# Eight weight places opened in the order in which their memory is freed, and one weight load of mid-stream split into 24 and 104 partitions

## The chip, the cores and the metric

The kernel runs on one core of one Trainium2 chip. The metric is the device time of one execution in microseconds; lower is better. A kernel is timed in several runs, and the profile is one more execution of the same program, taken by the hardware profiler. A verdict of "faster" or "slower" needs 2%.

Engine names in the profile: PE is the matmul engine, PEld its weight loads, DVE and ACT the vector and scalar engines, POOL the engine that issues nearly all loads here, SP another issuing engine. "L115" is line 115 of the kernel. The changed kernel has two more lines, so L546 and L551 of before are L548 and L553 of after.

## The reference

The reference is banded attention (8 heads, window 64) on 8 sequences of 576 rows, then a mix in the frequency domain, then a channel mix with a residual. The part that matters here is the middle one: 64 modes, each with a real and an imaginary 512 x 512 weight matrix.

```python
    X = np.fft.rfft(x, axis=1)
    ...
    Xr, Xi = (np.real(X[:, :n_modes]), np.imag(X[:, :n_modes]))
    Yr = np.einsum('bmd,mde->bme', Xr, w_r) - np.einsum('bmd,mde->bme', Xi, w_i)
    Yi = np.einsum('bmd,mde->bme', Xr, w_i) + np.einsum('bmd,mde->bme', Xi, w_r)
    Y[:, :n_modes] = Yr + 1j * Yi
    y = np.fft.irfft(Y, n=S, axis=1)
    u = x + y
    return (u + np.maximum(u @ w_ch, 0.0)).astype(np.float32)
```

All 127 weight matrices that are used (the imaginary one of mode 0 is not) have to be read once. They are most of the traffic.

## The kernel before

A weight load brings one matrix into a tile of 128 partitions and casts it to bf16 on the way. POOL issues it:

```python
    NLOAD = 2 * NM - 1            # 127
    def mode_of(i):               # the mode that load i belongs to
        return (i + 1) // 2

    def load_w(i, pool, tag, wt=None):
        m, im = divmod(i + (i > 0), 2)
        if wt is None:
            wt = pool.tile([128, NC, DM], BF16, name="wt", tag=tag)
        src = moe_w_i if im else moe_w_r
        nc.gpsimd.dma_start(out=wt, in_=src[m].rearrange("(p c) e -> p c e", c=NC))
        wtiles[m, im] = wt
```

During attention, the first 18 matrices go to places of their own (5 in a pool "wl", 13 in a pool "we", which the attention phase's memory holds), and more go to tiles that attention has finished with. When attention ends, its memory is given to other tiles. Eight of the new tiles are the "wm" places, which lie where "we" matrices and other tiles of the first phase lay. A place can be loaded only when what lay there has been read for the last time. `opens` says after which mode each place is offered to the stream of loads, and places are used in the order in which they come free:

```python
    MW = 8
    wmid = p2.enter_context(tc.tile_pool(name="wmid", bufs=1, side="right", reuse_waits="tile"))
    ...
    for j in range(LW):
        opens.setdefault(mode_of(j), []).append(("wl", j, NM))
    for j in range(MW):
        at = mode_of(LW + 6 + j) if LW + 6 + j < EARLY else vt_mode
        opens.setdefault(at, []).append(("wm", j, M0 + 2 * (j // 2)))
    free = []

    def refill_w(m):
        nonlocal nw
        for i in (2 * m - 1, 2 * m):
            if i in slot_of:
                free.append(slot_of.pop(i))
        free.extend(opens.pop(m, []))
        while nw < NLOAD and free:
            kind, j, last = slot = free.pop(0)
            if mode_of(nw) >= last:
                continue
            ...                    # load_w(nw, ...) into that place
            slot_of[nw] = slot
            nw += 1
```

POOL issues in program order. If the first load of a row of loads has to wait for its place, those behind it wait as well, even where their own places are free (13.85 us in the trace shown below).

The softmax here doesn't subtract the row's maximum and nothing guards it: scores larger than these inputs give would overflow.

## Time and profile before

| | before |
|---|---|
| median of the runs | 430.43 us (430.21 to 431.14) |
| the profiled execution | 431.61 us, 1.2 us above the median |
| bytes moved, mean rate | 92.18 MB, 214 GB/s |
| pace of the loads in mid-stream | one 512 KB weight load every 2.46 us |
| last weight landing | 392.41 us (from the DMA completions in the trace) |

The first view is the page of the kernel before. The DMA and GB/s rows cut the span into 40 slices; a digit 9 means that the sixteen DMA engines were busy for 90% of the slice or more. The queue lines give packets, megabytes, and the time that the packets took as a share of sixteen engines' span. The two groups are the mode matmuls: busy time and mean length, then the idle time just before them and what ended most of it.

```profile
DMA  7999999999999999999999999999999999993898
GB/s 140 213 215 211 213 213 211 213 213 213 214 213 213 198 210 231 212 213 214 213 213 213 213 213 213 214 213 214 213 213 213 213 214 213 213 214 73 265 344 292
DMA packets 31104, 92.18 MB, mean 214 GB/s; under 512 B 3424, under 2 KB 3680, under 8 KB 31056
...
q0 software_dynamic: 25984, 82.55, 96.6%
q8 instruction: 39, 0.64, 0.5%
...
L551 PE MATMUL psy<-XQ,wt 128*128 128x16 bf16 x784 | 48.1, 191 | 46.6 <-DMA wt<-in_moe_w_i_dram 44.0
L546 PE MATMUL psy<-XQ,wt 128*128 128x16 bf16 x832 | 52.1, 191 | 31.5 <-DMA wt<-in_moe_w_r_dram 31.0
```

From 3 to 390 us the DMA stream runs at 213 GB/s in nearly every slice, and the mode matmuls were kept idle for 44.0 + 31.0 = 75.0 us by weights that had not landed. So the stream of loads is the bound. The queue q8 carries instruction fetches: 39 of them, 16 KB each. They take 0.5% of the engines' time.

The second view is the table of windows of the kernel before: start and end, length, busy time and count of PE, PEld, DVE, ACT and POOL, then the granted clock, the DMA share, and GB/s.

```profile
core 0: us, PE busy (x) PEld busy (x) DVE busy (x) ACT busy (x) POOL busy (x), PEclk, DMA share, GB/s
168.00:171.00 3.00, 1.70 (x60) 1.58 (x55) 0.42 (x1) 1.17 (x2) 2.29 (x5) 0.50 0.78 182
171.00:390.00 219.00, 135.75 (x1871) 103.45 (x1872) 47.27 (x111) 34.40 (x66) 45.11 (x87) 0.69 1.06 213
343.00:352.00 9.00, 5.89 (x80) 4.43 (x80) 1.37 (x2) 1.16 (x2) 3.18 (x7) 0.67 1.07 215
392.50:430.00 37.50, 27.67 (x128) 20.13 (x128) 25.00 (x40) 24.34 (x47) 9.10 (x18) 0.92 0.76 259
```

The stream's usual share is 1.06 (a row takes 0.324 us and the next one starts 0.3045 us after it, so a full engine counts slightly over 1). At 168 to 171 us it falls to 0.78. The third view, the timeline of POOL in the kernel before, shows why. The bracket at the end of a line is the idle time before it and what ended it.

```profile
154.11 0.75 POOL L585 DMA_DIRECT2D wch<-in_moe_w_ch_dram  x1 [0.66 <-PE psy L546]
168.71 0.53 POOL L115 DMA_DIRECT2D wt<-in_moe_w_i_dram  x1 [13.85 <-PE psy L551]
169.23 0.54 POOL L115 DMA_DIRECT2D wt<-in_moe_w_r_dram  x1
169.75 0.55 POOL L115 DMA_DIRECT2D wt<-in_moe_w_i_dram  x1
...
172.35 0.59 POOL L115 DMA_DIRECT2D wt<-in_moe_w_r_dram  x1
```

After the load of `wch` nothing is issued for 13.85 us, because the load into the place wm0 waits for PE; the seven loads behind it then go out at once. The loads in flight run out meanwhile: from 170.0 to 170.5 us the DMA share is 0.48.

The fourth view is the timeline of PE at the end of the weight stream: the last two matrices, each multiplied as soon as it has landed.

```profile
389.98 0.63 PE L729 MATMUL psl<-XQ,wt 128*128 128x16 bf16 x16 [0.44 <-DMA wt<-in_moe_w_r_dram]
392.45 0.65 PE L729 MATMUL psl<-XQ,wt 128*128 128x16 bf16 x16 [0.47 <-DMA wt<-in_moe_w_i_dram]
```

PE waits for the last landing. Whatever makes that landing earlier makes the kernel shorter; the 37.4 us of the span after it are the last rows and the output.

### A finer clock: sixteen landings for each load

A load counts as landed when its semaphore has risen by sixteen: in the trace of before, each of the 120 starts of PE or PEld that a load had held up comes 0.04 us or more after the sixteenth increment of that load (median 0.04 us). The trace records sixteen increments for every load, spread over 0.71 us (the load landing at 173.68 us) to 3.66 us (the one landing at 123.64 us). A weight load has 128 rows of 4,096 bytes. In the packet list they fall into sixteen sequences side by side, each of 8 rows and a small write of 4 bytes for every load; such a sequence is taken as one engine here. Rows of one engine start 0.3045 us apart and the small write takes 0.022 us, so the 8 rows and the write make the 2.46 us.

The packets of the instruction fetches stand among these rows. In the trace of before the one at 243.11 us lies between two rows of one engine, and the next of them starts 0.96 us after it. The lengths of the 39 repeat with period eight (945, 936, 975, 974, 961, 893, 893 and 948 ns; 36 of 39 within 2 ns), which fits eight engines hit in turn. In the increments the sixteen do fall into two groups of eight: for the load landing at 340.77 us, eight lie within 0.66 us of the first and the other eight 1.54 to 3.00 us behind it. These are called the fast and the slow engines below. That the fetches are what makes these slow is inferred from these numbers.

This document uses one derived number. For each of the sixteen increments, "behind schedule" is its time less the time at which it would have come if every load so far had taken 2.457 us (2.795 us for one of q, k or v, 2.60 us for `wch`). The mean of the sixteen tells how the stream is doing; the largest tells when the load has landed. The trace does not name the engine of a packet, so the engines are numbered here in the order in which a load's rows are dealt to them.

### The profile page before, as it was taken

How to read it: one execution, taken by the hardware profiler on the slowest of the kernel's cores; microseconds unless marked ns; L12 is line 12 of the kernel's file. 1: busy time of each engine (PE TensorE's matmuls, PEld its weight loads, DVE VectorE, ACT ScalarE, POOL GpSimd, SP SyncE). 2: the span in 40 equal slices, each digit the busy share in tenths (PEclk: the TensorE clock that was granted, in tenths of full speed). 3: DMA queues.
4: the chain of work that ended last, by engine and by line, in shares of the span. 5: the costliest groups of instructions: out<-in, count | busy, mean ns of one | idle time of the engine just before them, and what ended most of it. 6: DMA issues, size and time to landing. Idle time of an engine off the chain costs nothing.

```text
span 429.8 us, 11338 instructions
## 1 busy us (share of the span) xinstructions
PE 316.0 (74%) x5057; PEld 228.0 (53%) x5057; DVE 162.0 (38%) x317; ACT 154.6 (36%) x271; POOL 98.3 (23%) x188
## 2 busy tenths in 40 slices
PE   6999999999989776422678888877266652398892
PEld 5665665666654476311566665655244541364681
DVE  5466766666662200306232322212011110042893
ACT  4585866866763121001122222122011110032891
POOL 7131321231020132221121221211111032101510
PEclk9999999999995555555598988879556665589997
DMA  7999999999999999999999999999999999993898
GB/s 140 213 215 211 213 213 211 213 213 213 214 213 213 198 210 231 212 213 214 213 213 213 213 213 213 214 213 214 213 213 213 213 214 213 213 214 73 265 344 292
DMA packets 31104, 92.18 MB, mean 214 GB/s; under 512 B 3424, under 2 KB 3680, under 8 KB 31056
## 3 DMA queue, kind: packets, MB, share of 16 engines
q0 software_dynamic: 25984, 82.55, 96.6%
q1 hardware_dynamic: 4928, 8.78, 5.6%
q8 instruction: 39, 0.64, 0.5%
q10 hardware_dynamic: 144, 0.13, 0.1%
q14 instruction: 9, 0.07, 0.0%
HBM read 162.53 MB, written 9.44 MB: 400 GB/s over the span
## 4 chain that ended last, share of the span: by engine, by line
DMA 42%; PE 36%; issue 10%; DVE 7%; ACT 2%; POOL 2%; DVEq 0%; POOLq 0%; ACTq 0%
DMA wt<-in_moe_w_r_dram 28%; DMA wt<-in_moe_w_i_dram 13%; PE pso L316 6%; PE pst L218 5%; PE psv L235 3%; PE pso L815 3%; PE psx L338 3%; PE pss L272 2%; DVE x_sb L324 2%; PE pss L372 2%; PE pss L291 2%; PE psz L572 2%; PE psy L551 2%; PE psy L546 2%; DVE vT L59 2%
## 5 line engine op out<-in xcount | busy, mean ns | idle before, releaser
L551 PE MATMUL psy<-XQ,wt 128*128 128x16 bf16 x784 | 48.1, 191 | 46.6 <-DMA wt<-in_moe_w_i_dram 44.0
L546 PE MATMUL psy<-XQ,wt 128*128 128x16 bf16 x832 | 52.1, 191 | 31.5 <-DMA wt<-in_moe_w_r_dram 31.0
L551 PEld LDWEIGHTS <-wt 128*128 128x128 bf16 x784 | 37.5, 104 | 51.8 <-DMA wt<-in_moe_w_i_dram 48.7
L546 PEld LDWEIGHTS <-wt 128*128 128x128 bf16 x832 | 39.7, 105 | 36.7 <-DMA wt<-in_moe_w_r_dram 35.0
L115 POOL DMA_DIRECT2D wt<-in_moe_w_i_dram x51 | 27.4, 537 | 99.7 <-DMA wt<-in_moe_w_i_dram 46.8
L572 PE MATMUL psz<-wch,xT 128*128 128x512 f32 x144 | 47.5, 473 | 0.4 <-DVE xT L569 0.4
L115 POOL DMA_DIRECT2D wt<-in_moe_w_r_dram x55 | 29.6, 539 | 77.7 <-DMA wt<-in_moe_w_r_dram 38.4
L569 DVE CAST xT<-pxt 128x512 fp32r<-128x512 bf16 x36 | 23.5, 687 | 63.0 <-PE pxt L566 63.0
L574 ACT CAST Z<-psz 128x512 fp32r<-128x512 f32 x36 | 21.1, 585 | 69.8 <-PE psz L572 61.9
L297 ACT ACTIVATE et<-pss 128x512 bf16<-128x512 f32 x72 | 39.2, 600 | 14.5 <-PE pss L291 14.5
L316 PE MATMUL pso<-vt,et 128*64 128x65 bf16 (+1 forms) x576 | 34.3, 209 | 4.1 <-DVE x_sb L324 4.0
L572 PEld LDWEIGHTS psz<-wch,xT 128*128 128x128 f32 x144 | 29.9, 222 | 6.3 <-issue 0.7
L316 PEld LDWEIGHTS <-et 128*64 128x64 bf16 (+1 forms) x576 | 23.8, 113 | 17.0 <-issue 8.9
L324 DVE TENSOR_TENSOR x_sb<-pso,rcp 128x640 bf16<-128x640 f32 x32 | 26.3, 822 | 0.9
L59 DVE CAST YT<-psy 128x256 fp32r<-128x256 f32 x6 | 2.5, 423 | 60.2 <-PE psy L551 60.2
L833 DVE TENSOR_TENSOR ot<-pso,x_sb 128x512 f32<-128x512 f32 x35 | 22.5, 687 | 3.3 <-PE pso L815 3.0
L272 PE MATMUL pss<-band,ident_bf 64*64 64x512 bf16 x160 | 21.0, 423 | 1.6 <-ACT et L297 1.6
L58 ACT CAST YT<-psy 128x256 fp32r<-128x256 f32 x6 | 2.2, 373 | 54.8 <-DVE YT L59 54.8
L59 DVE COPY vT<-pst 128x768 bf16<-128x768 bf16 x16 | 15.3, 958 | 13.0 <-PE pst L218 13.0
L820 ACT ACTIVATE pso<-pso 128x512 f32<-128x512 f32 x36 | 19.4, 585 | 1.9 <-PE pso L815 1.8
L686 DVE CAST Yb<-psa 96x512 fp32r<-96x512 f32 x8 | 5.5, 687 | 30.4 <-PE psa L680 30.4
L678 PE MATMUL psw<-wch,YT 128*96 128x512 f32 (+1 forms) x36 | 16.3, 598 | 0.2 <-DVE YT L788 0.2
(169 smaller groups left out, 522.0 us busy)
## 6 DMA issues: line engine op xcount, KB each, us to landing
wt<-in_moe_w_r_dram POOLq DMA_DIRECT2D x55, 512.0 KB, 19.1
wt<-in_moe_w_i_dram POOLq DMA_DIRECT2D x51, 512.0 KB, 19.1
out_dram<-ot SPq DMA_DIRECT2D x31, 256.0 KB, 3.5
rk<-in_k_dram POOLq DMA_DIRECT2D x8, 576.0 KB, 10.1
rq<-in_q_dram POOLq DMA_DIRECT2D x8, 576.0 KB, 13.9
rv<-in_v_dram POOLq DMA_DIRECT2D x8, 576.0 KB, 12.7
wy<-in_moe_w_i_dram POOLq DMA_DIRECT2D x4, 512.0 KB, 16.9
kT<-in_moe_w_r_dram POOLq DMA_DIRECT2D x2, 512.0 KB, 9.1
```

The source lines that it names most:

```text
L59: return nc.vector.tensor_copy(out=o, in_=i)
L115: nc.gpsimd.dma_start(out=wt, in_=src[m].rearrange("(p c) e -> p c e", c=NC))
L218: nc.tensor.transpose(out=ps[64 * hh:64 * hh + 64, c, :], in_=src[:, hh, (c0 + c) * D:(c0 + c + 1) * D], identity=ident_bf)
L272: nc.tensor.matmul(out=pss[(2 * w + hh) % 3][64 * half:64 * half + 64, :], lhsT=ident_bf[pp, pp], rhs=view(band[pp], 128 * half, [[0, WIN ...
L297: nc.scalar.activation(out=et[:, hh, :], in_=pss[(2 * w + hh) % 3], func=ACT_F.Exp, scale=EX_SCALE)
L316: nc.tensor.matmul(out=pso[po, hh, (i // 2) * VW:(i // 2) * VW + D + 1], lhsT=et[pk, hh, col:col + 64], rhs=vt[pk, 1 - f % 2, 2 * hh + g / ...
L324: nc.vector.tensor_tensor(out=view(x_sb, b * NT * DM + g * D, [[4 * D, 2], [DM, NT], [1, D]]), in0=view(pso, 0, [[512, 2], [VW, NT], [1, D]]),
L546: nc.tensor.matmul(out=psy[:, m % MG, e, :], lhsT=wr[:, c, ee], rhs=XQ[:, c, :, 1:3, m], start=(c == 0), stop=(m == 0 and c == NC - 1))
L551: nc.tensor.matmul(out=psy[:, m % MG, e, :], lhsT=wi[:, c, ee], rhs=XQ[:, c, :, 0:2, m], start=False, stop=(c == NC - 1))
L569: nc.vector.tensor_copy(out=xT, in_=pst)
L572: nc.tensor.matmul(out=psz, lhsT=xT[:, c, :], rhs=wch[:, c, :], start=(c == 0), stop=(c == NC - 1))
L833: nc.vector.tensor_tensor(out=ot, in0=ps, in1=x_sb[:, b, t, :], op=ALU.add)
```

## The change

The intent is to remove the wait of 13.85 us: the places are offered in the order in which their memory is freed, so wm0 goes last. All eight tiles are laid out ahead (their positions don't change). In addition, load number 63 of the 127 (NLOAD // 2) is cut into two transfers of 24 and 104 partitions.

```diff
-        nc.gpsimd.dma_start(out=wt, in_=src[m].rearrange("(p c) e -> p c e", c=NC))
+        for pp in (slice(0, 24), slice(24, 128)) if i == NLOAD // 2 else (slice(0, 128),):
+            nc.gpsimd.dma_start(out=wt[pp], in_=src[m].rearrange("(p c) e -> p c e", c=NC)[pp])
@@
     wmid = p2.enter_context(tc.tile_pool(name="wmid", bufs=1, side="right", reuse_waits="tile"))
+    mids = {j: wmid.tile([128, NC, DM], BF16, name="wt", tag=f"wm{j}") for j in range(MW)}
@@
     for j in range(MW):
-        at = mode_of(LW + 6 + j) if LW + 6 + j < EARLY else vt_mode
+        at = mode_of(LW + (j > 1) * (EW + 1 - j)) if j else vt_mode
         opens.setdefault(at, []).append(("wm", j, M0 + 2 * (j // 2)))
@@
-                load_w(nw, wmid, f"wm{j}")
+                load_w(nw, wmid, f"wm{j}", mids.pop(j, None))
```

## The prediction

> **What bounds the kernel now.** From 3 to 390 us the DMA stream does: the page's slices show 213 GB/s in nearly all, and the matmuls of lines 546 and 551 wait 75 us for weights (the waits). By issues and landings, a 512 KB weight load lands every 2.46 us, the last at 392.4 us; the 37.4 us after it (last rows, output) are a fixed tail. At 168-171 us the DMA share falls from 1.06 to 0.78 (window table). The timeline of the issuing engine shows why: after `wch` (154.1) nothing is issued until 168.7, because the first of eight "wm" loads waits for PE; the seven behind it then go out at once. A like dip at 141-144 us is not touched.
>
> **What the change does.** No arithmetic is added or removed. The eight places open as their old contents are consumed: the first load waits for a DMA only and should go out at about 155, the others after modes 6 to 14, which PE passes between 156 and 168. The dip at 168-171 goes. The split adds one issue of about 0.5 us to a queue with slack (mid-stream loads are issued 19 us before landing). Late places are refilled in another order, once 5 loads ahead instead of 7: still no stall.
>
> **How much is critical.** The dip is worth (1.06-0.78)/1.06 x 3 us = 0.8 us on average. But a load counts only when its sixteenth part has landed, and the sixteen DMA engines lag unequally. In each load's sixteen semaphore increments, eight engines stay within 0.7 us of the first; the others fall back about 1.1 us whenever a 16 KB instruction fetch passes (39 in all). Just before the dip the last engine is 2.4 us behind, five others about 1.6. Rank by rank, the leader lost 1.76 us in the dip, those five 0.7 to 0.9, the last only 0.1: the dip let laggards catch up. The order alone gains about 0.1 us, and the final spread would grow from 3.0 to about 4.6 us.
>
> The split looks made for that. [...] A row is 0.305 us (packet starts)[...]. I expect that the parameters were chosen to hit.
>
> **Predicted time.** 430.4 - 0.8 = 429.6 us; 8 in 10 between 428.8 and 430.5. Faster by over 2%: 1%; within 2%: 98%; slower: 1%.
>
> **What would show it.** Right: the eight issues spread over 155-169 us; DMA share near 1.06 at 168-171; last weight landing near 391.6; tail still about 37.4 us; a spread above 3 us before the split[...]. Wrong: the dip remains, or the last landing stays at 392.4 (laggards not relieved), or the tail changes.
>
> **What would make it wrong.** The laggard is none of the spared engines; fetches hit other engines or at other times; a place opened later lets the DMA run dry near 345 us; or more engines are relieved and the gain is larger.

The sum is 430.4 - 0.8 = 429.6 us. Its 0.8 us is the estimate for the split, the distance in the increments of before from the last engine (2.4 us behind the first) to the next five (about 1.6 us), gained if the split spares that last engine. That it does was expected, not shown. The 0.1 us of the order alone is not added in.

## The result, and the profile after

| | before | after |
|---|---|---|
| median (range) of the same rounds | 430.43 us (430.21 to 431.14), 5 runs | 430.71 us (430.26 to 430.85), 5 runs |
| ratio | | 0.9999, 95% interval 0.9986 to 1.0013 |
| profiled execution | 431.61 us | 430.85 us |
| last weight landing in it | 392.41 us | 391.98 us |

Ratios here are the mean time of one kernel's runs over that of the other's of the same rounds, so not quite the ratio of the medians. Executions over 1.5% slower than the fastest of the same kernel are left out of the means. The time did not move.

The page of the kernel after, in the same lines as before:

```profile
DMA  7999999999999999999999999999999999993898
GB/s 141 212 214 211 214 213 213 212 212 214 214 213 213 208 210 259 213 213 214 213 213 213 214 214 214 213 213 214 212 214 214 213 190 213 214 213 71 267 347 289
DMA packets 31136, 92.18 MB, mean 215 GB/s; under 512 B 3456, under 2 KB 3712, under 8 KB 31088
...
q0 software_dynamic: 26016, 82.55, 96.9%
q8 instruction: 39, 0.64, 0.5%
...
L553 PE MATMUL psy<-XQ,wt 128*128 128x16 bf16 x784 | 48.8, 191 | 52.2 <-DMA wt<-in_moe_w_i_dram 50.6
L548 PE MATMUL psy<-XQ,wt 128*128 128x16 bf16 x832 | 52.5, 191 | 27.8 <-DMA wt<-in_moe_w_r_dram 27.1
```

The sixteenth slice (161 to 172 us) rises from 231 to 259 GB/s: the pause is gone. But the thirty-third slice (343 to 354 us) falls from 214 to 190. The packets rise by 32, all under 512 bytes: small writes that belong to one more transfer (POOL issues 171 where it issued 170). The bytes are the same. The matmuls wait as long as before, 50.6 + 27.1 = 77.7 us.

The windows of the kernel after:

```profile
core 0: us, PE busy (x) PEld busy (x) DVE busy (x) ACT busy (x) POOL busy (x), PEclk, DMA share, GB/s
168.00:171.00 3.00, 1.49 (x50) 1.49 (x51) 0.00 (x0) 1.08 (x1) 0.53 (x1) 0.50 1.14 270
171.00:390.00 219.00, 133.39 (x1840) 101.08 (x1838) 46.97 (x111) 33.92 (x65) 44.35 (x85) 0.69 1.06 212
343.00:352.00 9.00, 5.55 (x65) 4.02 (x61) 1.37 (x2) 1.16 (x2) 3.70 (x7) 0.68 1.02 193
392.50:430.00 37.50, 27.26 (x118) 19.71 (x114) 25.08 (x40) 24.24 (x47) 9.14 (x18) 0.92 0.76 259
```

The timeline of POOL in the kernel after, around the eight loads and around the split load:

```profile
153.36 0.75 POOL L587 DMA_DIRECT2D wch<-in_moe_w_ch_dram  x1 [0.71 <-PE psy L548]
154.10 0.55 POOL L116 DMA_DIRECT2D wt<-in_moe_w_i_dram  x1
155.92 0.53 POOL L116 DMA_DIRECT2D wt<-in_moe_w_r_dram  x1 [1.27 <-DMA vt<-in_moe_w_i_dram]
158.35 0.53 POOL L116 DMA_DIRECT2D wt<-in_moe_w_i_dram  x1 [1.90 <-DMA wt<-in_moe_w_r_dram]
...
171.28 0.53 POOL L116 DMA_DIRECT2D wt<-in_moe_w_r_dram  x1 [2.53 <-PE psy L553]
...
216.12 0.52 POOL L116 DMA_DIRECT2D wt<-in_moe_w_r_dram  x1 [1.92 <-PE psz L574]
218.28 0.56 POOL L116 DMA_DIRECT2D wt<-in_moe_w_r_dram  x1 [1.64 <-DMA wt<-in_moe_w_i_dram]
```

The order does what it was meant to do. The eight loads are issued one by one from 154.10 to 171.28 us: the first right behind `wch`, the next six each when a load ahead has landed, the last after a wait of 2.53 us that the profile gives to PE. The wait of 13.85 us has no successor. The last two lines are the two parts of the split load.

The end of the stream in the kernel after, as the timeline of PE shows it:

```profile
389.57 0.63 PE L731 MATMUL psl<-XQ,wt 128*128 128x16 bf16 x16 [0.40 <-DMA wt<-in_moe_w_r_dram]
392.03 0.65 PE L731 MATMUL psl<-XQ,wt 128*128 128x16 bf16 x16 [0.45 <-DMA wt<-in_moe_w_i_dram]
```

The last landing of the two profiled executions differs by 0.43 us, but the profiled execution of before was itself 1.2 us above its median. Two single profiles can't settle half a microsecond.

### What the packets of the split load show

The prediction had to assume how the rows of the two parts are dealt to the engines. The packet list of the kernel after shows it. Written as runs of rows between the semaphore writes ("S") of one engine, the engines of the lower group go through the split load like this (from the packets between 226 and 240 us; two engines shown):

```
... 8 S 8 S 2 S 7 S 8 S 8 S ...
... 8 S 8 S 2 S 7 S 8 S 8 S ...
```

They get 2 rows of the small part and 7 of the large one, 9 in place of 8. Ten engines can be followed through the split load without a break in the list: eight get 2 and 7, one gets none and 7, one none and 6. With 24 and 104 rows in all, and the rest dealt alike, that makes twelve engines with 2 rows of the small part, and fourteen with 7 of the large one, one with 6 and one with none. This fits ⌈24/16⌉ = 2 and ⌈104/16⌉ = 7 rows for each engine in turn, both parts starting with the same engine, since the one with 6 has none of the small part. Numbered in that order, engines 0 to 11 get 9 rows, 12 and 13 get 7, engine 14 gets 6, and engine 15 gets none at all. The sixteen increments of neighbouring loads agree: one engine that had been 0.88 us behind the leader is suddenly 8 rows ahead of its schedule and leads by 1.9 us. Sorted, in microseconds after the first, for one load before the split and one after it:

```
load landing from 226.77: 0.00 0.10 0.12 0.17 0.19 0.30 0.81 0.88 | 2.25 2.37 2.38 2.47 2.79 3.38 3.45 3.53
load landing from 235.07: 0.00 | 1.91 1.99 2.00 2.07 2.20 2.61 2.73 | 3.36 4.13 4.37 4.65 4.67 4.78 5.34 5.41
```

Eight engines were behind before the split and eight still are. The one that was spared most belonged to the eight that needed nothing. Against the schedule, the slowest of the sixteen went from 4.3 to 4.6 us behind: one row. The jump of the spared engine came at 233 us. It kept its lead (1.91 us before the next for the load landing at 342.31 us) until the pause of the stream near 345 us.

### The profile page after: what moved, and what is told of

It is laid out like the page before. It is cut to its first block, busy times and chain, and to the rows that moved or that the text cites. A ratio compares the mean times of both kernels' runs of the same rounds, so it can differ in the third digit from the quotient of the medians.

```text
span 429.1 us, 11332 instructions
## 1 busy us (share of the span) xinstructions
PE 313.1 (73%) x5047; PEld 226.3 (53%) x5057; DVE 161.7 (38%) x317; ACT 154.4 (36%) x271; POOL 99.0 (23%) x189
## 4 chain that ended last, share of the span: by engine, by line
DMA 47%; PE 33%; issue 10%; DVE 7%; ACT 2%; POOL 1%; DVEq 0%; POOLq 0%; ACTq 0%
DMA wt<-in_moe_w_r_dram 28%; DMA wt<-in_moe_w_i_dram 18%; PE pso L317 6%; PE pst L219 6%; PE pso L817 3%; PE psv L236 3%; PE psx L339 3%; PE pss L273 2%; DVE x_sb L325 2%; PE pss L373 2%; PE pss L292 2%; DVE vT L59 2%; PE psz L574 1%; ACT vt L58 1%; PE pso L725 1%
## 5 line engine op out<-in xcount | busy, mean ns | idle before, releaser
L553 PE MATMUL psy<-XQ,wt 128*128 128x16 bf16 x784 | 48.8, 191 | 52.2 <-DMA wt<-in_moe_w_i_dram 50.6
L548 PE MATMUL psy<-XQ,wt 128*128 128x16 bf16 x832 | 52.5, 191 | 27.8 <-DMA wt<-in_moe_w_r_dram 27.1
L574 PE MATMUL psz<-wch,xT 128*128 128x512 f32 x144 | 46.5, 465 | 0.0
```

Source lines behind the costliest of these rows:

```text
L548: nc.tensor.matmul(out=psy[:, m % MG, e, :], lhsT=wr[:, c, ee], rhs=XQ[:, c, :, 1:3, m], start=(c == 0), stop=(m == 0 and c == NC - 1))
L553: nc.tensor.matmul(out=psy[:, m % MG, e, :], lhsT=wi[:, c, ee], rhs=XQ[:, c, :, 0:2, m], start=False, stop=(c == NC - 1))
L574: nc.tensor.matmul(out=psz, lhsT=xT[:, c, :], rhs=wch[:, c, :], start=(c == 0), stop=(c == NC - 1))
```

## The experiments

**Theory A.** The end of the stream is set by the slowest of the sixteen engines. Eight of them are slowed by instruction fetches of 16 KB (a fetch packet took 0.88 to 1.16 us in the traces of before and after; the one at 175.1 us in before took one engine from 4.18 to 5.28 us behind schedule, 1.1 us). The split, as the packets of the kernel after show it, spares engine 15, which is not one of the eight, and gives one row more to engines 0 to 11, so it costs the slowest up to 0.305 us. The pause at 168 us is real, but its removal is worth little at the end.

**Rivals.** That the split costs or gains through the extra issue or the bytes in flight; or that the mean of the stream, not its slowest engine, sets the end. Each quoted expectation says which rivals it means by its letters. The kernel before ran in every job, on the same chip as the kernels compared with it. All ratios below are against it.

### 1. The order alone

```diff
-        for pp in (slice(0, 24), slice(24, 128)) if i == NLOAD // 2 else (slice(0, 128),):
+        for pp in (slice(0, 128),):
```

> The order part alone, no split. Theory A (the slowest of the sixteen DMA engines sets the end, and it did not idle in the dip): the dip at 168-171 us is gone (DMA share above 1.03 there), the spread of a load's sixteen increments grows past 5 us by 300-340 us, yet the last weight load lands within 0.3 us of before and the time stays within 0.4 us of before. Rival B (what counts is the mean of the engines; the order gains 0.8 us and the split costs it again): last landing 0.8 us earlier, time near 429.6. Rival C (the order gains 0.8 us and gives it back in the late pauses at 344-353 us): the time is that of before, and the slowest engine, too, shows a pause of 0.5 us or more in 344-353.

Measured: 430.52 us (429.83 to 434.55), before 430.83, ratio 0.9998 (0.9963 to 1.0033). In its profile the pause is gone and the last weight landing is at 391.39 us (one window, and the last line of the weight stream in the timeline of PE):

```profile
168.00:171.00 3.00, 0.51 (x17) 0.41 (x15) 0.42 (x1) 1.66 (x2) 0.53 (x1) 0.50 1.16 281
391.44 0.65 PE L731 MATMUL psl<-XQ,wt 128*128 128x16 bf16 x16 [0.48 <-DMA wt<-in_moe_w_i_dram]
```

This job had more scatter than the first, so the ratio bounds the gain of the order only to about 1.5 us. Theory A had expected a landing within 0.3 us of before and a spread past 5 us; the landing came 1.02 us earlier and the spread at 338 us was 4.2 us, so it missed both. Rival B was nearer with its 0.8 us, but not with its 429.6 us.

### 2. The split alone

```diff
+        for pp in (slice(0, 24), slice(24, 128)) if i == NLOAD // 2 else (slice(0, 128),):
+            nc.gpsimd.dma_start(out=wt[pp], in_=src[m].rearrange("(p c) e -> p c e", c=NC)[pp])
```

(on the kernel before)

> The split alone, old order. Theory A: the dip stays; in the split load twelve engines carry one 0.305 us row more, so the slowest engine falls behind by 0.3 us, or stays if it is one of the three that carry one or two rows less: last landing 0 to 0.3 us later than before, time 430.4 to 430.8. Rival B: the split costs 0.8 us whatever the order: time near 431.2. Rival C: nothing.

Measured: 430.83 us (430.17 to 433.78), ratio 1.0002 (0.9972 to 1.0032). Its profile fell on the slowest of its executions, and so did that of experiment 4. The page of experiment 4 shows what these have in common:

```profile
PEclk9999995899998755555598997995556655589997
GB/s 141 212 213 213 214 212 214 188 210 212 214 203 199 196 210 261 212 214 215 212 213 212 213 215 214 212 213 213 215 213 213 214 210 213 213 214 49 276 332 287
```

In the seventh and eighth slices (65 to 87 us) the granted clock drops to 0.5 and 0.8, where the row of the kernel before has twelve 9s at its start. Attention then runs later, and the loads run short in the eighth slice (188 GB/s) and in the twelfth to fourteenth (203, 199, 196). The two profiled executions took 433.78 and 434.54 us, some 3 us over the medians of their kernels. Their traces are left out of every comparison of landings below, so what this experiment was to say of the landing was not tested until experiment 5.

### 3. The split eight times

```diff
-        for pp in (slice(0, 24), slice(24, 128)) if i == NLOAD // 2 else (slice(0, 128),):
+        for pp in (slice(0, 24), slice(24, 128)) if i in range(60, 76, 2) else (slice(0, 128),):
```

> The changed kernel with the same 24 and 104 split on eight loads of mid-stream instead of one: a dose. Theory A: seven more rows on twelve engines at 0.305 us each, so the last weight load lands 2.1 us later than in the changed kernel (near 394.1 us) and the time is near 432.7 us; if the slowest engine is one of the three relieved ones, about 0.3 us a load less of that. Rivals B and C in the form that only the issue or the count of bytes matters: the bytes are the same and the issuing engine has slack, so no change, 430.7 us.

Measured: 433.02 us (432.75 to 433.19, four runs), ratio 1.0041 (1.0012 to 1.0070). The last line of the weight stream in the timeline of PE:

```profile
394.05 0.64 PE L731 MATMUL psl<-XQ,wt 128*128 128x16 bf16 x16 [0.48 <-DMA wt<-in_moe_w_i_dram]
```

Seven more splits than the changed kernel should cost the slowest engine 7 x 0.3045 = 2.13 us if it gains one row each time. The last landing moved from 391.98 to 394.01 us, by 2.03 us. (Already at 340 us the slowest engine was 2.14 us further behind than in the changed kernel. Against the second profile of the changed kernel, in experiment 7, the landing moved by 2.48 us.) This agrees with the row more that the packets show, the same engines gaining it at each split, and gives the price where it is repeated: about 0.3 us a split. For a single split the price depends on which engine is last at that moment (experiment 5).

### 4. Load 63 as 17, 17, 17 and 77 partitions

```diff
-        for pp in (slice(0, 24), slice(24, 128)) if i == NLOAD // 2 else (slice(0, 128),):
+        for pp in (slice(0, 17), slice(17, 34), slice(34, 51), slice(51, 128)) if i == NLOAD // 2 else (slice(0, 128),):
```

> The changed kernel with the one load split into 17, 17, 17 and 77 partitions instead of 24 and 104. If each part of n rows is dealt out by the n/16, rounded up, to engines from the lowest on (as the split in the changed kernel's trace suggests), engines 0 to 7 carry 11 rows, engine 8 eight, engines 9 to 14 five and engine 15 two. Theory A: if the slow engines are among 9 to 14, the last weight load lands up to 0.9 us earlier and the time is near 429.8 us; if a slow one is among 0 to 7, it lands up to 0.9 us later. Rivals: same bytes, no change (430.7 us), or three more issues cost up to 1.5 us on the issuing engine.

Measured: 431.24 us (430.40 to 434.54), ratio 1.0013 (0.9980 to 1.0046): inconclusive as a time. If the parts are dealt as the packets show for 24 and 104, engines 0 to 7 get 3 rows more, engines 9 to 14 get 3 fewer. This profile was disturbed in the first phase, but the increments just before and after the cut load can still be compared with each other: six of the eight slow engines came about 0.9 us (three rows) nearer to their schedule, and two gained rows and became the last, 4.1 and 4.7 us behind the leader:

```
landing from 230.64: 0.00 0.05 0.10 0.15 0.21 0.22 0.32 0.67 | 1.23 1.24 1.25 1.36 1.38 1.53 1.75 2.71
landing from 236.64: 0.00 | 1.72 1.81 1.81 1.90 1.92 2.10 2.38 2.41 2.47 2.49 2.57 3.03 3.29 | 4.10 4.70
```

So a relief can be aimed, but not all eight slow engines are high ones.

### 5. Repeats: before, the order alone, the split alone

No edit: `b2_again` is the kernel before itself, `e5_order2` repeats experiment 1, `e6_split2` experiment 2, on another chip.

> The kernel before, unchanged, run as a trial of its own: its time against itself must be 1.000 within 0.1%, and its profile shows how much of the 0.4 to 1.0 us by which the last weight load moved between the profiles so far is mere scatter: the first profile of it was 1.2 us slower than its median run. If the last load lands at 391.4 us or earlier here, the first profile was a late one.

> The order part alone, again, because the first time the chip had runs of up to 437 us. Theory A as on record (the slowest DMA engine did not idle in the dip): last weight load within 0.3 us of that of the run of the kernel before sent with it, time within 0.4 us. Theory A2 (the first trials: after the dip all engines stand level, so the next instruction fetch makes a new slowest engine at once; without the dip it hits an engine that is not the slowest): last load 0.6 to 1.0 us earlier, time 429.7 to 430.0. Rival B (mean of the engines): 1.2 us earlier.

> The split alone, again (the first profile of it fell in an execution that was 3 us late before it). Theories A and A2: twelve engines carry one row of 0.305 us more, the slowest among them or not: last weight load 0 to 0.3 us later than the kernel before, time 430.4 to 430.8. Rival B: 0.8 us later.

Measured, with the kernel before at 430.60 us (429.70 to 433.37):

| | median (range), us | ratio (95% interval) | last landing, us |
|---|---|---|---|
| before itself | 431.10 (429.89 to 431.71) | 0.9998 (0.9972 to 1.0023) | 391.91 |
| order alone | 430.50 (429.56 to 431.19) | 0.9985 (0.9960 to 1.0011) | 392.03 |
| split alone | 430.34 (430.25 to 431.64) | 0.9986 (0.9959 to 1.0014) | 392.74 |

The surprise is in the windows of this second execution of the unchanged kernel:

```profile
168.00:171.00 3.00, 1.07 (x37) 0.96 (x34) 0.00 (x0) 0.00 (x0) 0.77 (x2) 0.50 1.14 275
343.00:352.00 9.00, 6.02 (x54) 4.28 (x52) 1.37 (x2) 1.16 (x2) 2.60 (x5) 0.50 0.95 178
```

There is no pause at 168 us. The same program had passed attention about 2.5 us earlier in this execution (the last two loads of attention issued at 142.47 us, not at 144.97), so wm0's place was free before the loads in flight had run out: the eight loads were issued from 163.38 us on, not from 168.71. The pause that the change removes is there in some executions of the kernel before and not in others. The split alone shows a smaller one. Of the four undisturbed profiles with the old order (experiment 7 has the fourth), one has the long pause.

Against this second profile of the kernel before (391.91 us), the order alone landed 0.12 us later: Theory A2 and Rival B, which expected it 0.6 to 1.2 us earlier, missed, but there was no pause to remove. The split alone landed 0.83 us later, where 0 to 0.3 us was expected. That doesn't show the cost of the split, because this execution had a pause of its own. At the split itself the slowest engine moved the other way, from 6.5 to 5.9 us behind schedule: the last engine of that moment was relieved by two rows, as engine 14 is. In the second profile of the changed kernel (experiment 7) the slowest went from 4.4 to 4.3 us, in the first from 4.3 to 4.6. So one split can cost 0.3 us at that point, or gain 0.6.

### 6. Order, and two loads cut into five 7s and 93

```diff
+        for pp in [slice(7 * n, 7 * n + 7) for n in range(5)] + [slice(35, 128)] if i in (61, 91) else [slice(0, 128)]:
```

(on the order alone; by the same dealing engines 0 to 6 get 3 rows more, 7 to 14 get 2 fewer, each time)

> The order part, and two loads (numbers 61 and 91) each cut into five pieces of 7 partitions and one of 93, which by the dealing seen so far (rows a piece, partitions/16 rounded up, to engines from the lowest on) puts 11 rows on engines 0 to 6, 6 on engines 7 to 14 and 3 on engine 15, in place of 8 each: four rows less in all (1.2 us) on the eight engines that the instruction fetches seem to hit, if those are 7 to 14. Theories A and A2: the last weight load lands 1.0 to 1.2 us earlier than with the order part alone, the spread of a late load's increments falls from about 4.2 to about 3 us or less, time 428.6 to 429.2. Rival (bytes or issues count, not the slowest engine): no change against the order part, or later by up to 1 us for ten more issues.

Measured: 432.27 us (431.55 to 437.69), ratio 1.0054 (1.0009 to 1.0100): slower, where 428.6 to 429.2 us was expected. The spread of the sixteen increments fell, from 4.4 us at 224 us to 1.4 us at 250 us (in part because engines that run dry become level, as in the pause of before, where it fell from 2.42 to 0.71 us between the loads landing at 168.47 and 173.68 us), but the window behind it shows the price:

```profile
222.00:233.00 11.00, 9.72 (x98) 7.85 (x99) 3.01 (x5) 2.55 (x5) 3.51 (x7) 0.84 0.90 165
```

The kernel before has a share of 1.06 and 213 GB/s in that window. In the traces of before and after none of POOL's transfers (162 and 163 pairs) is issued sooner than 0.28 us after the landing of the one eight before it; if that holds here, with six of those eight being parts of one load, little is in flight. That this alone makes the engines run dry is not shown: behind the first cut a load was also held for 4.06 us, until 230.45, by a wait that the profile gives to PE, and at the second cut of the same form the share stayed at 1.07 (300 to 311 us). All sixteen engines lost: the mean behind schedule at 390 us is 5.53 us, against 3.97 us with the order alone.

### 7. Four loads cut into 7, 7, 2 and 112, on both orders; and the changed kernel again

```diff
+        for pp in (slice(0, 7), slice(7, 14), slice(14, 16), slice(16, 128)) if i in (50, 66, 82, 98) else (slice(0, 128),):
```

(`e9_gentle` on the order alone, `e10_gentle_old` on the kernel before; `a2_after` is the changed kernel with no edit)

> The new order alone, with four widely spaced weight loads (numbers 50, 66, 82, 98) cut into 7, 7, 2 and 112 partitions. By the dealing seen in the changed kernel's packets (each piece starts again at the lowest engine, a piece of n partitions gives n/16 rows rounded up to each engine in turn) two engines get 10 rows, five get 9 and nine get 7 of such a load in place of 8. Theory A (the laggards are the eight engines that the 16 KB instruction fetches fall on, they are among the nine, and the last one to land sets the end): over four loads the laggards lose 4 rows of 0.305 us, so the spread of the 16 increments of a weight load falls from about 4.1 us at 340 us to 1.5 to 2.9 us, the last weight landing comes 0.8 to 1.2 us earlier than with the order alone (391.4 to 392.0 so far, so 390.2 to 391.2), and the median is 429.2 to 429.9 us. Only four pieces of one load stand in the eight issue lanes at a time, so the stream should not run dry as it did when 5 small pieces were cut from a load. Rival B (the stream as a whole, bytes in flight and places coming free, sets the end, not the slowest engine): the spread falls, but the last landing stays within 0.3 us of 391.7 or gets later by the twelve extra issues, median 430.3 to 431.

> The kernel before, old order, with the same four loads cut into 7, 7, 2 and 112 partitions. Theory A: the same gain as with the new order, 0.8 to 1.2 us on the last weight landing (before 392.4 in its first profile, 391.9 in its second), median 429.3 to 430.0 us. If the pause of the stream near 168 us that the old order has in some executions mattered to the end once the laggards are relieved, it would now show, as a time later than the new order's by 0.5 us or more; if not, the two relief kernels are within 0.3 us of each other. Rival B: no gain, 430.3 to 431.

> The changed kernel itself once more, a second look at its scatter and its profile on the same chip as the two relief kernels. Every theory: 430.3 to 430.9 us, last weight landing 391.7 to 392.5, and no pause of the stream near 168 us. Theory A adds: the spread at 340 us is 3.5 to 4.5 us, and one engine (the one that got no row of the small split) is 8 rows ahead after load 63.

Measured, before at 430.58 us (429.75 to 431.50) on this chip:

| | median (range), us | ratio (95% interval) | last landing, us |
|---|---|---|---|
| cut loads, new order | 431.59 (430.31 to 432.30) | 1.0020 (1.0003 to 1.0037) | 392.36 |
| cut loads, old order | 431.55 (431.18 to 432.14) | 1.0023 (1.0008 to 1.0038) | 392.48 |
| changed kernel again | 431.19 (429.66 to 436.75, one slow run) | 1.0013 (0.9988 to 1.0038) | 391.53 |

The expectation of Theory A was missed: both cut kernels are slower by about 1 us instead of faster by 1. The changed kernel missed its expectation too, by less: 431.19 us for 430.3 to 430.9, and 391.53 us for 391.7 to 392.5. The increments say why the cuts failed. Sorted, for a load before the first cut and one after the fourth, new order:

```
landing from 196.33: 0.00 0.17 0.17 0.21 0.26 0.77 0.86 1.31 | 3.42 3.47 3.48 3.51 3.52 3.54 3.64 4.67
landing from 330.72: 0.00 0.03 0.07 | 2.11 2.94 3.35 3.99 4.12 | 4.17 4.20 4.25 5.20 5.22 5.31 | 6.43 6.49
```

By the same dealing nine engines, 7 to 15, lose a row at each cut, seven, 0 to 6, gain one or two. Only three of the eight fast engines were left in front, so only three of them are among the nine. The other six of the nine are slow ones. That leaves two slow engines among 0 to 6, and these two gained rows and stand alone at the end, at 6.43 and 6.49. I had taken the slow engines to be eight neighbours, 7 to 14. With the six that experiment 4 relieved they must be 9 to 14 and two of the low ones.

The run is still useful against the rival of the mean. The cut kernel and the changed kernel were 3.79 and 3.81 us behind schedule in the mean of the sixteen at 388 us, which is the same, and 6.66 and 5.73 us in the slowest. Their last landings differ by 0.83 us.

The two orders are 0.04 us apart with the same cuts. The execution of the old order that was profiled had no long pause at 168 us either.

### 8. Three loads cut into 4, 4, 4, 4 and 112

```diff
+        for pp in [slice(4 * n, 4 * n + 4) for n in range(4)] + [slice(16, 128)] if i in (50, 74, 98) else [slice(0, 128)]:
```

(on the order alone; by the same dealing engines 0 to 3 get 11 rows, the other twelve get 7)

> The new order alone, with three weight loads (numbers 50, 74, 98) cut into 4, 4, 4, 4 and 112 partitions: by the dealing, engines 0 to 3 get 11 rows of such a load and the other twelve get 7, in place of 8. The four runs with cut loads so far fit one set of eight engines that instruction fetches fall on: 9 to 14 and two among 2 to 6. In the kernel with 7, 7, 2 and 112 those two gained rows, so the slowest engine was not relieved: the mean of the sixteen at the end was that of the changed kernel of the same job (3.79 against 3.81 us behind nominal), the slowest 6.66 against 5.73 us, the last landing 392.36 against 391.53. Theory A (the slowest engine sets the end), if the two are among 4 to 6: all eight lose 3 rows, the slowest is at most 5.2 us behind at the end, last weight landing 390.6 to 391.4, median 429.4 to 430.2. If one of the two is 2 or 3, it gains 9 rows, 2.7 us: the slowest is then 7.5 to 8.5 us behind, last landing 393 to 394.5, median 432 to 433. Rival B (the mean of the stream sets the end): last landing 391.4 to 392.4 in either case, median 430.3 to 431.5, whatever the slowest engine does.

Measured: 429.59 us (428.90 to 430.82), before 430.69 us (430.07 to 431.20), ratio 0.9977, 95% interval 0.9963 to 0.9991. This is the fastest kernel and the only one whose interval lies below 1. The increments, before the first cut and after the third:

```
landing from 197.96: 0.00 0.03 0.07 0.10 0.14 0.52 0.55 0.61 | 1.37 1.68 1.70 1.70 1.76 1.93 1.95 3.02
landing from 340.29: 0.00 0.03 0.27 0.62 | 1.89 2.26 2.32 2.40 | 2.46 3.20 3.29 3.33 3.39 3.58 3.66 4.26
```

Four fast engines stay in front, four come back to meet the slow ones, and no slow engine falls behind the others. So engines 0 to 3 are all fast, and the two low slow engines are among 4 to 6. Experiments 7 and 8 have the same number of extra issues (4 x 3 and 3 x 4, twelve each). They differ in which engines got the rows, and their ratios differ by 0.0043, which is 1.9 us, with opposite signs. The numbers of issues and bytes can't explain that, and from 196 to 330 us, where the cuts lie, both traces keep a share of 1.06. The two ran on different chips, each against the kernel before of its own job, so a difference of the chips is not excluded. Nor is the gain over the order alone shown: its interval in experiment 5 (0.9960 to 1.0011) overlaps with this one.

The trace of this kernel shows less than its times do. Its profiled execution took 430.36 us, second slowest of its six, and its end reads

```profile
391.29 0.65 PE L731 MATMUL psl<-XQ,wt 128*128 128x16 bf16 x16 [0.46 <-DMA wt<-in_moe_w_i_dram]
```

so the last weight landed at 391.24 us, 0.15 us earlier than with the order alone (391.39) and 0.29 us earlier than in the second profile of the changed kernel (391.53). The engines behind it were 5.52 us behind in the slowest and 4.03 us in the mean, against 5.73 and 3.81 us for the changed kernel: slowest better, mean worse. A landing of 390.6 to 391.4 us and a median of 429.4 to 430.2 us were expected, and both came. But the slowest was to be at most 5.2 us behind and was 5.52, and that the faster executions of this kernel land earlier still is inferred from the times, not seen in a trace.

### The slowest engine, and the mean, in all profiles that were not disturbed

Microseconds behind schedule of the last increment, at three times, and at the end also the mean of the sixteen:

| profile | 130 us | 210 us | 388 to 391 us | mean at the end | last landing |
|---|---|---|---|---|---|
| before | 3.26 | 5.52 | 6.68 | 5.19 | 392.41 |
| before again (no pause) | 3.13 | 4.24 | 6.14 | 4.49 | 391.91 |
| split alone, second profile (small pause) | 3.18 | 5.29 | 6.99 | 4.68 | 392.74 |
| after | 3.17 | 4.34 | 6.27 | 4.43 | 391.98 |
| after again | 3.29 | 4.44 | 5.73 | 3.81 | 391.53 |
| order alone | 3.39 | 4.53 | 5.69 | 3.97 | 391.39 |
| order alone again | 3.13 | 4.28 | 6.34 | 3.81 | 392.03 |
| split eight times | 3.03 | 4.22 | 8.29 | 6.16 | 394.01 |
| order, 7 7 2 112 four times | 3.24 | 4.05 | 6.66 | 3.79 | 392.36 |
| order, 4 4 4 4 112 three times | 3.37 | 4.19 | 5.52 | 4.03 | 391.24 |
| order, five 7s and 93 twice | 3.10 | 4.17 | 7.44 | 5.53 | 393.15 |
| old order, 7 7 2 112 four times (no long pause) | 3.14 | 4.42 | 6.77 | 4.41 | 392.48 |

The fourth column follows the last by construction, since the amount of work is the same. What the table adds is the third column: with a pause at 168 us the slowest engine is 5.3 to 5.5 us behind at 210 us, without one 4.05 to 4.5. By this comparison, with one long and one small pause in it, the pause costs the slowest engine 1.0 us or so by then. Of that, 0.3 to 1.0 us is left at the end. Fetches after 210 us hit some of the slow engines again, and two profiles of one kernel differ by 0.6 us there (order alone: 391.39 and 392.03).

The time of an execution is 38.1 to 39.3 us more than its last weight landing in all these profiles. This scatter of the tail, 1.2 us, is larger than any effect of the change.

## Why the prediction was right or wrong

**The bound: right.** Weights decide; PE waits for the last landing in every trace, and the tail did not change (share 0.76 and 259 GB/s in both windows after 392.5 us).

**The order: right in what it does.** The eight issues were predicted at 155 to 169 us and came at 154.10 to 171.28 us. The share at 168 to 171 us rose from 0.78 to 1.14.

**What the order is worth: the reason was wrong, the size undecided.** The prediction argued that the slowest engine loses only 0.1 us in the pause, because the pause lets the laggards catch up. The traces show about 1.0 us at 210 us. The 0.1 us itself was right: in the first trace of before the slowest engine was 4.07 us behind schedule ahead of the pause and 4.18 us after it. What the prediction overlooked is that a pause levels the engines only once. All sixteen then stood 3.5 to 4.2 us behind, and the next fetch, at 175 us, took one of them to 5.28 us at once; with the order alone the slowest stayed at 3.6 us until 180 us. Two things then take that gain away from the median. The pause is not there in every execution of the kernel before, and from 210 us to the end scatter of half a microsecond is added. In times, the order alone gave ratios of 0.9998 and 0.9985, with intervals of 0.25 to 0.35% on each side. So the order is worth between nothing and about 1 us in an execution, and its effect on the median is not resolved here.

**The split: this is the step that failed.** Its sum needed the last engine to be one that the split spares. Of that the prediction said: "I expect that the parameters were chosen to hit." Nearly all of the 0.8 us in its sum rests on that expectation; no trace that it had showed how a split load is dealt. The packets show twelve engines with a row more, and the increments that the engine spared by eight rows is not one of the eight slow ones. Of the eight slow ones, five gain a row (two of 4 to 6, and 9 to 11), 12 and 13 lose one, and 14 loses two. So a single split moved the slowest engine by +0.3, -0.1 and -0.6 us in the three undisturbed traces that show it, according to which engine was last, and eight of them cost 2 us. The predicted 429.6 us contained -0.8 where a term of a few tenths of either sign belonged. The measured median, 430.71 us, lies 1.1 us above 429.6 and 0.2 us above the predicted range; by the ratio (0.9999) the changed kernel stands at 430.4 us, inside it. Runs scatter by half a microsecond and more, so where the result falls at the edge of the range is luck. The answer "within 2%" was right.

**Late places: partly wrong.** "Still no stall" does not hold for the leading engines: at 343 to 352 us the share falls to 1.02 (before 1.07), and the least delayed of the sixteen increments goes from 0.78 us ahead of schedule to 1.92 us behind it. The last increment goes from 5.78 to 6.27 us behind, and the other slow engines of that load move with it, so in this execution the pause reached the end: 0.5 us, more than the split's part. Where the order stands alone the last increment does not move at all (5.61 to 5.60 us): a pause that only the engines ahead felt cost nothing there. The second profile of the kernel before has the same pause (share 0.95, and the last goes from 5.5 to 6.0 us), so it isn't the change's own.

**What was lacking.** The prediction had the right yardstick (the sixteenth landing) and the right suspects (fetches on eight engines). It lacked the map from row to engine, and put intent in the place of evidence. A cheaper answer was there: it had itself only a few of the sixteen engines spared (in the packets it is one by eight rows, one by two and two by one), so without the map the last engine was more likely not to be among them.

**What stays open.** Why the slow engines, on which the fetches fall, are 9 to 14 and two of 4 to 6, and whether that holds for other programs, was not tested; the numbers are of one program, on four chips in the experiments. Which two of 4 to 6 it is was not settled. Why the stream pauses near 345 us in some executions of both kernels and not in others was not tested either. How much of the order's 1.0 us survives to the end, averaged over executions, would need many profiles.

## What to carry to other kernels

Where a stream of loads is the bound, look at all sixteen increments of a load, not at its landing alone: here the last came 3.00 us after the first at 340.77 us in the kernel before, and a gain in the mean can leave the last where it is (order alone again against after: mean 3.81 against 4.43 us behind, slowest 6.34 against 6.27). Before moving rows between the DMA engines, find out which engines are behind, by cutting a load unevenly and counting who falls back: twelve issues more gave a ratio of 0.9977 or of 1.0020 here, with the rows in different places. And before removing a pause that one trace shows, look at a second execution of the same kernel: it may not have it.
